# Strided sparse attention with a feed-forward layer: three normalizations on other engines, layer 1 begun with the strided pairs, transposes in two PSUM tiles

## The chip, the core and the metric

The kernel runs on one core of a Trainium2 chip. The core has five engines, each with its own queue, which it works through in order: TensorE (PE in the profile; PEld is its weight load), VectorE (DVE), ScalarE (ACT), GpSimd (POOL) and SyncE (SP). Sixteen DMA engines move data between HBM and the on-chip memory (SBUF); TensorE writes to PSUM, of which there are eight banks. [...] The metric is the device time of one execution in microseconds, median of several runs.

## The reference

```python
# q, k, v: 8 batches x 8 heads x 576 positions x 64; float32
scores = q @ k.T / sqrt(64)
rel = pos[:, None] - pos[None, :]
mask_local   = (rel >= 0) & (rel < 32)                                    # heads 0 to 3
mask_strided = (rel >= 0) & (pos[None, :] % 32 == pos[:, None] % 32)      # heads 4 to 7
attn = softmax(where(mask, scores, -1e9))
x = (attn @ v).transpose(0, 2, 1, 3).reshape(4608, 512)
h = x @ w_in                                      # 512 -> 2048
g = maximum(h, 0) + alpha * minimum(h, 0)         # alpha per column of h
out = g @ w_out                                   # 2048 -> 512
```

## The kernel before

**Attention.** Each batch has two units: the strided heads (4 to 7) and the local heads (0 to 3), two pairs of heads each. In the numbering of the code a batch's unit 0 is local (pairs `hp` 0 and 1) and its unit 1 is strided (pairs 2 and 3). Work is cut into pieces, and `pieces` (filled by `alone` and the loop at L559) is their order. A piece is one of:

- `T(u, "q")` or `T(u, "k")` (L234, `transpose_piece`): eight 128x128 transposes on TensorE, whose result is copied to `qT` or `kT`. For batches 0 and 1 ("early") the copy is done in two halves, one by VectorE and one by ScalarE. A k piece also has the last 64 positions (`tails`, L268), which it transposes first in the early batches.
- `Sc(g, i)` (L341) or `Sb(g)` (L290): half of the scores of pair g, or both halves. Scores go to PSUM, ScalarE takes the exponential into `et`. Every first half uses the double bank `sp`, of which there is one; every second half uses two of the banks that `hbank` deals out. In batch 0 the mask is added in PSUM by a matmul; in batch 1 VectorE multiplies by it (`run_masks`, L333), two pieces later or when the values of the pair want it.
- `Pv(g, a)` (L452): a group of the product with V, with one more column that holds the sum of the weights; then the normalization: on VectorE a reciprocal of the sums (L478) and a multiply (L480) into `x16`.
- `X(g)` (L485): transposes of `x16`, copied into `xT`, the input of layer 1. `xT[:, hp]` holds the 128 columns of pair `hp`, so the four k-slices (`kk`) of layer 1 are the four pairs.

**The feed-forward part** takes chunks of 512 tokens. `lin1_piece(n, m)` (L642) makes 128 of 2048 columns: four matmuls (`kk` 0 to 3) into a bank from `hbank`, a negative Relu on ScalarE (L662) and a combination on VectorE (L665), deferred by one step in `late`. There are three banks, `hb0` to `hb2`; the third joins the rotation (`turn`) when layer 1 begins. `lin2_piece(n, i)` (L671) is a quarter of a 128-token block: four matmuls; the fourth quarter ends with a copy `osb` on ScalarE (L684) and a store. From chunk 2 on layer 2 is done by `lin2_sums` (L738) with sums of quadrants in place of some products; the sums of weights are made once (`w_sums`, L699), the third of them at step 20 of chunk 2.

**Order.** Every instruction stays in the order of the program on its engine. The program begins with loads and with batch 0's pieces alone (loop at L890, 26 pieces); `warm` puts fillers between them, matmuls of zeros whose result nobody reads. Then come 16 pieces of layer 1 of chunk 0, then 16 parts of layer 2 of chunk 0 with batch 1's 22 pieces between them, as a list of numbers says (L930). From chunk 1 on the pieces of the next batch are spread over both layers.

**Buffers.** The pool `ps` has three PSUM banks for transposes, tails, values and outputs. A bank is given on when all its readers are done. `x16` has three buffers, `neg` (the negative Relu's output) three, `rc` (reciprocals) four.

**Queues for loads.** GpSimd issues most loads (L123 to L180, and the weights in `load_w`, L816) in the order of the program, between its own casts and copies: `cast_l` (float32 to float16 of the local q and k), `cast_v` (V of the strided heads), `over_v` (L202: an overlap of 32 positions between the blocks of local V).

The softmax here doesn't subtract the row's maximum and nothing guards it: scores larger than these inputs give would overflow.

## Time and profile before

| | |
|---|---|
| median of 7 runs | 305.46 us (305.21 to 306.19) |
| the profiled execution's own time | 305.46 us |
| its span | 303.6 us |
| TensorE busy | 295.1 us (97%) |
| VectorE, ScalarE, GpSimd busy | 221.9, 177.6, 170.4 us |
| granted TensorE clock | full in all of the 40 slices |
| layer 1 of chunk 0 | from 24.30 to 38.06 us |
| layer 2 of chunk 0, with batch 1's attention | from 38.06 to 61.15 us |

A row of the profile's groups reads: line, engine, operation, output and inputs, shape, count, busy time, mean of one, idle time before and what ended most of it. A line of the timeline has start, duration, engine, line, operation and the idle time of that engine before it with its releaser. The ends of matmuls are modelled; a run of them starts one about every 0.22 us (512 columns) though a single one is shown with 0.38.

### The profile page before, as it was taken

The numbers are of one execution on the slowest core, as the hardware profiler recorded it, in microseconds if no ns is written. First come the engines' busy times: TensorE is split into PE (matmuls) and PEld (weight loads), VectorE is DVE, ScalarE is ACT, GpSimd is POOL, SyncE is SP. The second block draws the span as 40 slices with busy tenths as digits, with TensorE's granted clock in tenths as the row PEclk, the third lists the DMA queues.
The fourth block names the chain that finished last, engine by engine and source line by source line (L and its number), as shares of the span: only waits on it lengthen the run. The fifth ranks groups of instructions, "written<-read, shape, count | busy, mean of one in ns | idle before, by whom it ended". The sixth has DMA issues, their size and how long they took to land.

```text
span 303.6 us, 7042 instructions
## 1 busy us (share of the span) xinstructions
PE 295.1 (97%) x2786; PEld 191.4 (63%) x2786; DVE 221.9 (73%) x417; ACT 177.6 (59%) x330; POOL 170.4 (56%) x176
## 2 busy tenths in 40 slices
PE   8799999999999999999999999999999999999995
PEld 3454455644555468746888887458845874684484
DVE  5686867758783889488848884888578958845872
ACT  3655764597547774677567765766477246516620
POOL 8872279847999874877397729771746003101300
PEclk9999999999999999999999999999999999999999
DMA  7999999999799982999399919961921080012004
GB/s 226 193 206 207 204 231 221 168 170 262 152 162 208 196 106 38 164 278 121 45 170 275 114 29 153 184 86 30 189 64 23 0 162 0 2 69 72 0 0 140
DMA packets 81201, 40.38 MB, mean 133 GB/s; under 512 B 58624, under 2 KB 76304, under 8 KB 81168
## 3 DMA queue, kind: packets, MB, share of 16 engines
q0 software_dynamic: 41728, 17.38, 48.6%
q1 hardware_dynamic: 39168, 22.03, 32.6%
q8 instruction: 22, 0.36, 0.6%
q10 hardware_dynamic: 272, 0.52, 0.5%
q14 instruction: 11, 0.09, 0.1%
HBM read 38.01 MB, written 9.44 MB: 156 GB/s over the span
## 4 chain that ended last, share of the span: by engine, by line
PE 87%; DVE 6%; DMA 2%; ACT 2%; issue 1%; SPq 0%; ACTq 0%
PE hb L652 41%; PE hb L771 25%; PE hb L679 8%; PE pv L469 4%; PE tp L250 2%; DMA kl<-in_k_dram 2%; PE sp L421 2%; PE opl L771 1%; DVE gsum L723 1%; DVE x L480 1%; PE xp L488 1%; DVE qT L190 1%; PE sph L421 1%; ACT kT L188 1%; PE hb L829 1%
## 5 line engine op out<-in xcount | busy, mean ns | idle before, releaser
L652 PE MATMUL hb<-xT,win 128*128 128x512 f16 (+1 forms) x640 | 132.0, 358 | 0.1
L665 DVE SCALAR_TENSOR_TENSOR gT<-neg,oma,hb 128x512 f16<-128x512 f32 x144 | 105.4, 744 | 36.2 <-ACT neg L662 28.3
L662 ACT ACTIVATE neg<-hb 128x512 f32<-128x512 f32 x144 | 86.0, 598 | 36.4 <-PE hb L652 35.8
L652 PEld LDWEIGHTS <-win 128*128 128x128 f16 x640 | 60.0, 98 | 54.6 <-issue 0.4
L436 POOL TENSOR_TENSOR et<-et,consts 128x576 f16<-128x576 f16 (+1 forms) x24 | 30.6, 1276 | 41.9 <-ACT et L434 41.8
L723 POOL TENSOR_TENSOR gsum<-gT 128x512 f16<-128x512 f16 x21 | 24.1, 1148 | 52.0 <-DVE gT L665 52.0
L771 PEld LDWEIGHTS <-gsum 128*128 128x128 f16 x448 | 41.6, 98 | 4.9 <-DVE gsum L723 0.2
L771 PEld LDWEIGHTS <-gT 128*128 128x128 f16 x336 | 31.5, 98 | 4.8
L480 DVE TENSOR_TENSOR x<-pv,rc 96x384 f16<-96x384 f32 (+2 forms) x62 | 33.0, 532 | 2.1
L443 POOL TENSOR_TENSOR et<-et,consts 128x576 f16<-128x576 f16 (+1 forms) x24 | 32.7, 1364 | 2.2 <-ACT et L440 2.2
L679 PE MATMUL hb<-wout,gT 128*128 128x512 f16 x128 | 32.3, 379 | 0.1
L469 PEld LDWEIGHTS <-et 72*128 72x128 f16 (+1 forms) x448 | 23.6, 98 | 10.9 <-issue 1.3
L783 ACT COPY o<-hb 128x512 f32<-128x512 f32 (+1 forms) x28 | 15.8, 565 | 24.1 <-PE hb L771 24.1
L771 PE MATMUL hb<-wout,gT 128*128 128x256 f16 x216 | 27.3, 273 | 0.0
L771 PE MATMUL hb<-wout,gsum 128*128 128x256 f16 x216 | 26.9, 273 | 0.0
L434 ACT ACTIVATE et<-sp 128x576 f16<-128x576 f32 (+1 forms) x24 | 15.5, 645 | 18.3 <-PE sp L421 18.3
L771 PE MATMUL hb<-wsum,gsum 128*128 128x256 f16 x216 | 26.0, 272 | 0.0
L786 DVE TENSOR_TENSOR o<-hb,o 128x512 f32<-128x512 f32 (+1 forms) x21 | 14.3, 679 | 14.7 <-PE hb L771 10.9
L478 DVE RECIPROCAL rc<-pv 72x6 f32<-72x6 f32 (+2 forms) x80 | 14.6, 182 | 10.0 <-PE pv L469 9.6
L440 ACT ACTIVATE et<-sph 128x288 f16<-128x288 f32 (+1 forms) x48 | 18.9, 409 | 0.0
L679 PEld LDWEIGHTS <-gT 128*128 128x128 f16 x128 | 10.7, 97 | 9.1
L469 PE MATMUL pv<-vs,et 72*128 72x65 f16 x256 | 15.5, 193 | 0.7 <-DVE vs L190 0.4
(103 smaller groups left out, 321.3 us busy)
## 6 DMA issues: line engine op xcount, KB each, us to landing
out_dram<-o SPq DMA_DIRECT2D x27, 256.0 KB, 3.8
kl<-in_k_dram SPq DMA_DIRECT2D x6, 512.0 KB, 8.4
ql<-in_q_dram SPq DMA_DIRECT2D x5, 512.0 KB, 8.2
stv<-in_v_dram POOLq DMA_DIRECT2D x8, 288.0 KB, 7.6
vl<-in_v_dram POOLq DMA_DIRECT2D x6, 384.0 KB, 10.0
win<-in_moe_w_in_dram POOLq DMA_DIRECT2D x4, 512.0 KB, 11.8
wout<-in_moe_w_out_dram POOLq DMA_DIRECT2D x4, 512.0 KB, 14.2
out_dram<-osb SPq DMA_DIRECT2D x8, 256.0 KB, 4.8
```

Of the source, the lines that this page charges most:

```text
L436: keep(nc.gpsimd.tensor_tensor(mv, mv, m, op=ALU.mult))
L440: keep(nc.scalar.activation(ev[:, n * y : n * y + n], sps[y][0:r, 0:n], AF.Exp, scale=SCALE))
L443: keep(nc.gpsimd.tensor_tensor(mv, mv, m, op=ALU.mult))
L469: keep(nc.tensor.matmul(pv[:, 65 * x : 65 * x + 65], et[0:r, c : c + 128], v16[0:r, 2 * P.pr + hh, t, :] if P.strided else v16[:, 6 * (2 * ...
L480: keep(nc.vector.tensor_tensor(P.x16[0:w, c0 : c0 + 64 * nb].rearrange("r (c e) -> r c e", e=64), pvv[:, :, 0:64], rc[0:w, 0:nb].unsqueeze ...
L652: keep(nc.tensor.matmul(hps[:, dst : dst + w], win16[:, kk, 128 * m : 128 * m + 128], xT[:, kk, src : src + w], start=(kk == 0 and x == 0) ...
L662: keep(nc.scalar.activation(neg, hps, AF.Relu, scale=-1.0))
L665: keep(nc.vector.scalar_tensor_tensor(gTs[n][:, m, :], neg, oma[:, m : m + 1], hps, op0=ALU.mult, op1=ALU.add))
L679: keep(nc.tensor.matmul(ops, gTs[n][:, kf, 128 * mt : 128 * mt + 128], wout16[:, kf, :], start=(kf == 0), stop=(kf == 15)))
L723: keep(eng.tensor_tensor(o[:, k0:k1], x[:, k0:k1], y[:, k0:k1], op=op))
L771: keep(nc.tensor.matmul(dst, lhs[:, kf, 128 * mt : 128 * mt + 128], rhs[:, kf, :], start=(first and own and kf == 0), stop=(kf == 7), skip ...
L783: keep(nc.scalar.copy(o, x))
```

## The change

1. *Transposes.* In batches 0 and 1 the eight transposes of a piece go into two PSUM tiles of four, and the copies are cut the same way: one engine copies the first four transposes for both pairs, the other the last four. Before, both engines read one tile, each for one pair.
2. *Normalizations.* In batch 0 the groups (pair 2, group 1), (pair 3, group 0) and (pair 0, group 0) are copied from PSUM to SBUF by ScalarE; the reciprocal stays on VectorE, the multiply is done by GpSimd. Both are put behind the next value piece's own normalization or ahead of the next output piece.
3. *Order of batch 0's pieces.* Local scores and values are interleaved differently, and the strided pairs' outputs come earlier.
4. *Layer 1.* In the last pieces of batch 0, layer 1's slices 2 and 3 (the strided pairs) of its first three column blocks are issued, then slice 0 of these; slice 1 follows in `lin1_piece`. The third bank joins before that. Four single fillers are left in the loop where there were fourteen.
5. *GpSimd's queue.* It casts both halves of batch 0's strided V, does `over_v` in two parts, and issues three of four output-weight loads and the loads of batch 1 behind the loop.
6. *Layer 2 of chunk 0.* The list of piece numbers is changed.
7. *Weight sum.* The third sum of weights is made in four quarters at steps 19, 21, 22 and 23.

```diff
@@ -199,10 +199,10 @@
                       "p (h t d) -> p h t d", h=2, t=8))
         cast16[(b, True, "v")] = v16
 
-    def over_v(b, eng):
+    def over_v(b, eng, lo=1, hi=24):
 
         v16 = vls[b % 2]
-        cast_copy(eng, v16[0:32, 1:24, :], v16[96:128, 0:23, :])
+        cast_copy(eng, v16[0:32, lo:hi, :], v16[96:128, lo - 1 : hi - 1, :])
 
 
     class Pair:
@@ -243,26 +243,26 @@
         dst = qTs[u % 2][:, :, 0:576] if nm == "q" else kTs[u % 2][:, :, 32:608]
         if early and nm == "k":
             tails(b, u, strided)
-        tp = pspool.tile([128, 8, 64, 2], F16, tag="ps", name="tp")
-        for j in range(8):
-            blk = (src[:, j % 2, 128 * (j // 2) : 128 * (j // 2) + 128] if strided
-                   else src[:, j].rearrange("p f d -> p (f d)"))
-            keep(nc.tensor.transpose(tp[:, j].rearrange("r p e -> r (p e)"), blk, ident))
-        if strided:
-            main = tp.rearrange("r j p e -> r e j p")
-            o = dst.rearrange("r e (j p) -> r e j p", j=8)[:, :, :, 0:64]
-        else:
-            main = tp.rearrange("r t p e -> r e p t")
-            o = dst[:, :, 0:512].rearrange("r e (p t) -> r e p t", t=8)
-        if early:
-            for e in range(2):
-                eng = "dve" if (nm == "q") == (e == 0) else "act"
-                if u == 0 and nm == "q":
-                    eng = "dve"
-                cast_copy(eng, o[:, e : e + 1], main[:, e : e + 1])
-            return
-        cast_copy("act", o, main)
-        if nm == "k":
+        halves = 2 if early else 1
+        nj = 8 // halves
+        for z in range(halves):
+            tp = pspool.tile([128, nj, 64, 2], F16, tag="ps", name="tp")
+            for x in range(nj):
+                j = nj * z + x
+                blk = (src[:, j % 2, 128 * (j // 2) : 128 * (j // 2) + 128] if strided
+                       else src[:, j].rearrange("p f d -> p (f d)"))
+                keep(nc.tensor.transpose(tp[:, x].rearrange("r p e -> r (p e)"), blk, ident))
+            if strided:
+                main = tp.rearrange("r j p e -> r e j p")
+                o = dst.rearrange("r e (j p) -> r e j p", j=8)[:, :, nj * z : nj * z + nj, 0:64]
+            else:
+                main = tp.rearrange("r t p e -> r e p t")
+                o = dst[:, :, 0:512].rearrange("r e (p t) -> r e p t", t=8)[:, :, :, nj * z : nj * z + nj]
+            eng = "act"
+            if early and (u == 0 and nm == "q" or (nm == "q") == (z == 0)):
+                eng = "dve"
+            cast_copy(eng, o, main)
+        if nm == "k" and not early:
             tails(b, u, strided)
 
     def tails(b, u, strided):
@@ -474,15 +474,33 @@
             late.pop(0)()
         w = P.w
         rc = rpool.tile([128, 8], F32, tag="rc", name="rc")
+        c0 = 128 * grp[0]
+        by_pool = P.b == 0 and (P.hp, a) in ((2, 1), (3, 0), (0, 0))
+        if by_pool:
+            st = npool.tile([128, 512], F32, tag="neg", name="pvs")
+            keep(nc.scalar.copy(st[0:w, 0 : 65 * nb], pv[0:w, 0 : 65 * nb]))
+            pv = st
         pvv = pv[0:w, 0 : 65 * nb].rearrange("r (c e) -> r c e", e=65)
-        keep(nc.vector.reciprocal(rc[0:w, 0:nb], pvv[:, :, 64]))
-        c0 = 128 * grp[0]
-        keep(nc.vector.tensor_tensor(
-            P.x16[0:w, c0 : c0 + 64 * nb].rearrange("r (c e) -> r c e", e=64),
-            pvv[:, :, 0:64],
-            rc[0:w, 0:nb].unsqueeze(2).to_broadcast([w, nb, 64]), op=ALU.mult))
+
+        def norm():
+            keep(nc.vector.reciprocal(rc[0:w, 0:nb], pvv[:, :, 64]))
+            keep((nc.gpsimd if by_pool else nc.vector).tensor_tensor(
+                P.x16[0:w, c0 : c0 + 64 * nb].rearrange("r (c e) -> r c e", e=64),
+                pvv[:, :, 0:64],
+                rc[0:w, 0:nb].unsqueeze(2).to_broadcast([w, nb, 64]), op=ALU.mult))
+
+        if not by_pool:
+            norm()
+        while later:
+            later.pop(0)()
+        if by_pool:
+            later.append(norm)
+
+    later = []
 
     def x_piece(P):
+        while later:
+            later.pop(0)()
         xp = pspool.tile([128, 1024], F16, tag="ps", name="xp")
         for t in range(P.n):
             keep(nc.tensor.transpose(
@@ -539,8 +557,12 @@
 
         if u0 == 1:
             fns = [T(u0, "q"), T(u0, "k"), Sc(A[0], 0), Sc(A[0], 1), T(u1, "q"), Sc(A[1], 0), T(u1, "k")]
-            fns += [Sc(A[1], 1), Sc(L[0], 0), Pv(A[0], 0), Sc(L[0], 1), Pv(A[0], 1), Pv(A[0], 2)]
-            fns += [Sc(L[1], 0), Pv(A[1], 0), Sc(L[1], 1), Pv(A[1], 1), Pv(A[1], 2)]
+            fns += [Sc(A[1], 1), Sc(L[0], 0), Pv(A[0], 0), Sc(L[0], 1), Pv(A[0], 1), Sc(L[1], 0)]
+            fns += [Pv(A[0], 2), Sc(L[1], 1), Pv(A[1], 0), Pv(A[1], 1), Pv(L[0], 0), Pv(A[1], 2)]
+            fns += [X(A[0]), Pv(L[0], 1), X(A[1]), Pv(L[1], 0), Pv(L[1], 1), X(L[0]), X(L[1])]
+            for fn in fns:
+                feed(fn, -1)
+            return
         else:
             fns = [T(u0, "q"), T(u0, "k"), Sb(A[0]), Sb(A[1])]
             fns += [Pv(A[0], 0), T(u1, "q"), Pv(A[0], 1), T(u1, "k"), Pv(A[0], 2), Sb(L[0])]
@@ -639,24 +661,35 @@
 
     gTs = {}
 
-    def lin1_piece(n, m):
-        if m == 0:
-            gTs[n] = gpool.tile([128, 16, 512], F16, tag="gT", name="gT")
+    hcur = {}
+
+    def lin1_mm(n, m, kks, first, last):
+        if first:
+            hcur[m] = hbank()
+        hps = hcur[m]
         c0 = (512 * n) % RING
         parts = [(c0, 0, min(512, RING - c0))]
         if c0 + 512 > RING:
             parts.append((0, RING - c0, 512 - (RING - c0)))
-        hps = hbank()
-        for kk in range(4):
+        for kk in kks:
             for x, (src, dst, w) in enumerate(parts):
                 keep(nc.tensor.matmul(
                     hps[:, dst : dst + w],
                     win16[:, kk, 128 * m : 128 * m + 128],
                     xT[:, kk, src : src + w],
-                    start=(kk == 0 and x == 0),
-                    stop=(kk == 3 and x == len(parts) - 1),
+                    start=(first and kk == kks[0] and x == 0),
+                    stop=(last and kk == kks[-1] and x == len(parts) - 1),
                     skip_group_check=True,
                 ))
+        return hps
+
+    def lin1_piece(n, m):
+        if m == 0:
+            gTs[n] = gpool.tile([128, 16, 512], F16, tag="gT", name="gT")
+        if n == 0 and m < 3:
+            hps = lin1_mm(n, m, (1,), False, True)
+        else:
+            hps = lin1_mm(n, m, (2, 3, 0, 1) if n == 0 else range(4), True, True)
 
         neg = npool.tile([128, 512], F32, tag="neg", name="neg")
         keep(nc.scalar.activation(neg, hps, AF.Relu, scale=-1.0))
@@ -696,7 +729,7 @@
 
         return wout16[:, 8 * i : 8 * i + 8, 256 * j : 256 * j + 256]
 
-    def w_sums(eng, which):
+    def w_sums(eng, which, k0=0, k1=8):
 
         w1, w2, w4 = wsum
         w3 = wq(0, 1)
@@ -708,7 +741,7 @@
         }
         for z in which:
             o, x, y, op = steps[z]
-            keep(eng.tensor_tensor(o, x, y, op=op))
+            keep(eng.tensor_tensor(o[:, k0:k1], x[:, k0:k1], y[:, k0:k1], op=op))
 
     def g_sum(eng, n, which, k0, k1):
 
@@ -873,12 +906,10 @@
     cast_l(0, "k")
     load_w(2, False)
     load_w(3, False)
+    cast_v(0, 0, "pool")
     cast_v(0, 1, "pool")
-    over_v(0, "pool")
-    for c in range(4):
-        load_w(c, True)
-    load_unit(1, True)
-    load_unit(1, False)
+    load_w(0, True)
+    over_v(0, "pool", 1, 12)
 
     warm(12)
     keep(nc.vector.tensor_copy(id16, ident[0:16, 0:16]))
@@ -892,13 +923,21 @@
             keep(nc.tensor.transpose(apt[:, 0:16], alpha_r, id16))
             keep(nc.vector.tensor_scalar(
                 oma, apt[:, 0:16], -1.0, 1.0, op0=ALU.mult, op1=ALU.add))
-        if i == 8:
-            cast_v(0, 0, "dve")
         attn_step(end0)
         if i < 2:
             warm(4 - i)
-        elif i > 8 and i not in (10, 13, 15):
+        elif i in (9, 11, 13, 16):
             warm(1)
+        if i == 13:
+            over_v(0, "pool", 12, 24)
+        if i == 21:
+            turn.append(2)
+        if i in (22, 23, 24):
+            lin1_mm(0, i - 22, (2, 3), True, False)
+    for c in range(1, 4):
+        load_w(c, True)
+    load_unit(1, True)
+    load_unit(1, False)
 
     def attn_n(n, end):
         for _ in range(n):
@@ -921,13 +960,14 @@
     cast_l(2, "k")
 
 
-    turn.append(2)
+    for m in range(3):
+        lin1_mm(0, m, (0,), False, False)
     for m in range(16):
         lin1_piece(0, m)
         attn_n(0, end1)
     for i in range(16):
         lin2_piece(0, i)
-        attn_n((0, 1, 1, 1, 1, 2, 1, 2, 1, 2, 1, 2, 2, 3, 2, 0)[i], end1)
+        attn_n((0, 0, 0, 1, 1, 2, 2, 2, 2, 2, 2, 2, 2, 2, 2, 0)[i], end1)
         if i > 13:
             attn_n(1, end1 + 2)
     assert pos["i"] == end1 + 2
@@ -954,8 +994,9 @@
                     w_sums(nc.vector, ({18: 1, 22: 2, 26: 4}[i],))
             else:
                 lin2_sums(n, i - 16)
-                if n == 2 and i == 20:
-                    w_sums(nc.vector, (3,))
+                if n == 2 and i in (19, 21, 22, 23):
+                    k0 = {19: 0, 21: 2, 22: 4, 23: 6}[i]
+                    w_sums(nc.vector, (3,), k0, k0 + 2)
             if n < B - 2 or i < 16 or i > 19:
                 acc += left / (22.5 if n == 1 else 16 if n == B - 2 else 20.5) * (0.5 if i < 16 else 1.0)
             cnt = int(acc)
```

## The prediction

> **What bounds the kernel now.** I read the page first.
>
> ```profile
> span 303.6 us, 7042 instructions
> ...
> PE 295.1 (97%) x2786; PEld 191.4 (63%) x2786; DVE 221.9 (73%) x417; ACT 177.6 (59%) x330; POOL 170.4 (56%) x176
> ```
>
> TensorE is the bound overall, but fillers count as busy there, so I cut the span at the stage borders with the table of stretches.
>
> ```profile
> 10.00:24.30 14.30, 12.81 (x190) 8.06 (x191) 10.48 (x28) 8.12 (x18) 10.10 (x14) 1.00 1.60 184
> 24.30:38.06 13.76, 13.76 (x64) 6.27 (x64) 10.66 (x15) 8.96 (x15) 3.79 (x6) 1.00 1.25 205
> 38.06:61.15 23.09, 22.18 (x262) 13.06 (x260) 15.96 (x38) 13.07 (x28) 19.52 (x22) 1.00 1.46 207
> 61.15:94.80 33.65, 33.65 (x297) 16.89 (x296) 23.59 (x43) 22.96 (x45) 26.28 (x24) 1.00 1.17 190
> ...
> 107.50:118.50 11.00, 10.69 (x115) 8.15 (x113) 10.10 (x18) 7.86 (x16) 5.26 (x6) 1.00 0.60 72
> ```
>
> The columns are stretch, sum, then PE, PEld, DVE, ACT, POOL. From 61.15 PE is full, but for 107.5 to 118.5. So the change can act in three places: the front (batch 0's attention, to 24.30), the shared stage (layer 2 of chunk 0 with batch 1's attention, 38.06 to 61.15), and near 118. What is gained or lost before 61.15 passes to the end undamped.
>
> In the front the timeline (start, duration, engine, line, what, idle before and its releaser) shows who is last:
>
> ```profile
> 15.78 0.19 DVE L478 RECIPROCAL rc<-pv 72x6 f32<-72x6 f32 x1 [0.43 <-PE pv L469]
> ...
> 23.79 0.46 DVE L190 COPY xT<-xp 128x576 f16<-128x576 f16 x1 [0.40 <-PE xp L488]
> ...
> 25.15 0.60 ACT L662 ACTIVATE neg<-hb 128x512 f32<-128x512 f32 x1 [1.44 <-PE hb L652]
> ...
> 25.78 2.48 DVE L665 SCALAR_TENSOR_TENSOR gT<-neg,oma,hb 128x512 f16<-128x512 f32 x3 [1.53 <-ACT neg L662]
> ```
>
> Between 15.78 and 23.41 VectorE runs ten normalizations almost without gap: 0.19 + 0.55 us for 384 elements, 0.17 + 0.42 for 256, so 8 x 0.73 + 2 x 0.59 = 7.0 of 7.6 us. It bounds the front. Layer 1 then takes 63 matmuls of 0.2184 from 24.30 to 38.06; the first piece's bank is free again at 25.78 + 0.74 (mean of the L665 row) = 26.5, just before the fourth piece's first matmul (24.30 + 11 x 0.2184 = 26.7).
>
> The timeline of the shared stage, and one line of the third place:
>
> ```profile
> 41.00 0.59 ACT L188 COPY qT<-tp 128x512 f16<-128x512 f16 x1 [2.30 <-DVE qT L190]
> ...
> 43.26 0.65 ACT L316 ACTIVATE et<-sp 72x576 f16<-72x576 f32 x1
> ...
> 43.80 0.70 ACT L320 ACTIVATE et<-hb 72x288 f16<-72x288 f32 x2
> ...
> 44.37 0.30 PE L308 MATMUL sp<-qT,kT 64*128 64x72 f16 x8
> ...
> 48.81 0.61 PE L250 MATMUL tp<-consts,kl 128*128 128x128 f16 x8 [0.35 <-ACT qT L188]
> ...
> 118.50 0.36 PE L469 MATMUL pv<-vs,et 72*128 72x65 f16 x6 [0.31 <-DVE x16s L480]
> ```
>
> The reader sees copies that wait for copies, exponentials that are 0.65 and 0.70 long, and TensorE idle behind ScalarE (0.35) and behind VectorE (0.31). The shared stage's PE work is 64 x 0.2165 (layer 2) + 4 x 0.45 and two tails of 0.17 (transposes) + two transposes of batch 2 (1.0) + 4 x 0.41 (scores) + 10 x 0.18 (values) + 4 x 0.26 (outputs) = 21.5; so 1.6 of 23.09 is stall. The two scores of a pair stand one layer-2 part apart (42.89, 44.37), and that part hides the exponentials.
>
> **What the Trainium skill says.** PSUM — Partial Sum Buffer, "PSUM bank collisions raise a hardware error": two engines must not touch one bank and quadrant at once, reads included. The trace agrees: ScalarE's half of a transpose's copy starts after VectorE's has ended (40.27 + 0.69, then 41.00); such waits sum to 5.6 and 4.2 us. GPSIMD Engine Reference, section 3, is used as a price below, with ScalarE: Activation LUTs, "What ACT_TABLE_LOAD costs": 186 ns + 0.833 per element; the trace's 512-element copy takes 0.59 where this gives 0.61.
>
> **The change, part by part.**
>
> *Transposes in two tiles.* The same matmuls and copies; the halves' copies no longer wait for each other (0.6 us each), but each half spans both heads of the pair, so scores now wait for both halves, where before the first pair waited for one. And a q and k transposition now takes five tiles (q, q, tail, k, k) of the three "ps" buffers instead of three. In the front, VectorE is held by ks and madd until 8.12 as before, its q half ends 8.80, tails 9.06; k's second half ends 10.02 against ScalarE's 10.15 before: first scores 10.05, gain 0.15. For the local unit: q halves from 11.7 (4 transposes are enough, before 12.09) to 12.95, k by 14.0, scores 14.03 against 14.34.
>
> *Cast of V to GpSimd.* 0.41 us off VectorE; on GpSimd 1.06 from 13.25 to 14.31, the other half to 15.37. First values at 14.6 instead of 15.40. Two split overlap copies (1.43 together) cost nothing: the first ends about 16.9, values of local pairs start at 18.4.
>
> *Three normalizations moved, new order.* Each takes 0.55 off VectorE and puts a copy on ScalarE (390 elements: 0.50, between the rows 0.59 for 512 and 0.41 for 288) and a multiply on GpSimd. The trace has no such multiply: masks of 576 take 1.28, sums of 512 1.15, so 2.0 ns per element and 0.12 fixed, 0.89 for 384; the GPSIMD page's 4497 ns for 2048 gives an estimate of 0.84. Range 0.8 to 1.3. Walking the queues from 14.6: scores of the second local pair end 17.67; its exponentials hold ScalarE to 18.45; only behind them comes the copy for the second moved one, 18.95; reciprocal behind VectorE's own work, 19.2; GpSimd has done the first multiply (17.7 to 18.6) and the second overlap copy (19.35), so this multiply is 19.35 to 20.25. That one is late next: pair 3's transposes 20.3 to 20.72, its copy to 21.4, the first new layer-1 group waits for that to 21.45, and the last pair's values, normalization (22.7), transposes (23.45) and copy (23.96) queue behind it. Without any such wait TensorE's own work from 14.2 on (4 fillers and six layer-1 matmuls, 10 x 0.217; 3 score halves x 0.58; ten values, 2.3 by the chain's 0.12 to 0.35; four outputs, 1.5: 7.7, where ten fillers fewer are minus 2.17 and the six plus 1.30) would end at 21.95. I take: nine layer-1 matmuls done and the last ones starting at 24.1, against 24.30.
>
> *Layer 1 with strided pairs first.* Saves no matmul, but 8 of the 63 behind 24.30, 1.75. That isn't all gained: three pieces finish within 0.65 and the fourth waits for the first's bank: 0.22 + 0.2 + 0.60 + 0.03 + 0.75 = 1.8 behind 24.1. Then 13 pieces x 0.866 = 11.25: end 37.2. Gain 38.06 - 37.2 = 0.9 (0.66 from the order, 0.2 from the start).
>
> *Loads behind the loop.* Three output-weight loads and ten of batch 1 (q, k, two tails and V of each unit) now issue behind GpSimd's last multiply (21.15) instead of from 18.3. The rows with "<-DMA win" and "<-DMA wout" (24.18, 26.71, 29.30, 31.83) show that the queue lands one weight load each 2.5 us in order, and the last weight load landed at 36.9. It is full until 29.30 with loads issued earlier, so the order and times of landing stay: nothing. Without that cover each us late would move batch 1's k (39.5).
>
> *Attention pieces in layer 2: (0,0,0,1,1,2,...).* Batch 1's start moves from part 1 to part 3: 37.2 + 4 x 0.87 = 40.7, against 39.63. Then both scores of a pair stand together: the second's first group needs the first exponential out of the double bank, 0.65 behind; its second needs the two banks, until 44.50 by the pattern 42.89/43.80/0.70. That is 1.0 us of stall which the part hid before. The next transposes come one part closer: k's first tile waits for q's VectorE half, behind masks and a normalization (0.75), its second for a normalization (0.5), against 0.35 and two short waits of 0.1 before: 0.7 more. The parallel copies and the missing wait for osb (43.41) give 0.2 back. Sum: +1.5 (0.5 to 2.0). With -0.9 that puts 61.15 at 61.8.
>
> *Weight sum in quarters.* Instead of one of 1.21 at 116.68, four of 0.43 (row of 512 elements). The idle 0.31 at 118.50 goes. But the last quarter stands behind the addition of its own part (119.83, 0.69), so ends about 120.6, while the group that reads it reaches the last two slices at 120.1: 0.5. Net +0.2 (-0.4 to +0.5).
>
> Sum: -0.9 + 1.5 + 0.2 = +0.8. The profiled execution took 305.46 (span 303.6 and 1.9 around), which is also the median. Forecast 306.3.
>
> **Rivals.** *The front is faster than my walk* (other side). If the moved copy and multiply aren't last, the last layer-1 matmuls can start as early as 22.6 (21.95 and three matmuls). Then layer 1 ends at 35.7, -2.4, and -2.4 + 1.5 + 0.2 = -0.7, 304.8. From a start before 23.3 on the change gains. For: in my walk GpSimd idles from 16.9 to 17.7, so it has room, and VectorE is no longer full. Against: ScalarE's queue of exponentials and copies.
> *The doubled pieces cost nothing.* If banks come free in another order than I take, +1.5 shrinks to 0.5: -0.9 + 0.5 + 0.2 = -0.2, 305.3, no change. Against: the exponentials' durations.
> *GpSimd becomes the bound.* At 1.3 per multiply, the second and third end 0.8 later; nothing hides it, as pair 3's transposes stand in front of all other TensorE work: +1.6, 307.1. For: VectorE masks took 2.02 a pair instead of 0.81 beside GpSimd casts. Against: the normalization's VectorE operand is in PSUM.
>
> **How the numbers follow.** About 0.2% (0.6 us) is what this kernel's measurement tells from no change. My forecast 0.45 (own range 305.7 to 307.0; a tenth of this lies within 0.2%), doubled pieces free 0.20, front faster 0.22 , GpSimd bound 0.13. Slower: 0.40 + 0.13 = 0.53; same 0.05 + 0.19 = 0.24; faster 0.22 + 0.01 = 0.23. Low end 304.3: the front case with the shared stage at +1.0. High end 307.4: GpSimd's case and a little of the unknown pattern of the copies.
>
> **What would show it.** The first layer-1 matmul that completes a piece at 24.1, an idle of about 1.2 before the fourth piece, layer 2 from 37.2; a wait of scores for ScalarE's exponentials of about 1 us near 45; transposes waiting for VectorE near 49; layer 1 of chunk 1 at 61.8; a wait on L711's successor near 120. I am wrong if the border at 61.15 moves forward, or if pair 3's transposes aren't kept by GpSimd.

## The result and the profile after

The changed kernel takes 306.96 us (median of 27 executions, 306.59 to 311.04) against 305.30 us before (median of 64). The ratio is 1.0082 with a 95% interval of 1.0065 to 1.0099. It lies above that of the medians (1.0054) because it follows the means, 308.05 against 305.55 us (the latter without two slow executions of 310.09 and 314.86). The executions of the changed kernel fall into groups that differ in the TensorE clock they were granted over the span.

| mean granted clock | executions | time |
|---|---|---|
| 0.998 and more | 15 | 306.59 to 307.11, median 306.82 |
| 0.992 to 0.994 | 8 | 308.31 to 309.77, mean 308.9 |
| 0.988 to 0.989 | 4 | 310.79 to 311.04 |

Below, an execution is at full clock when this mean is 0.998 or more. The kernel before is at full clock in all but one of the 84 executions that were measured beside the experiments. So two things are to be explained: 1.5 us at full clock (306.82 - 305.30), and some 2.1 us more for each step down in clock.

The profiled execution is one of the group with the lowest clock (311.04 us). The head of the page, TensorE's row and the granted clock:

```profile
span 309.3 us, 7033 instructions
...
PE 296.3 (96%) x2776; PEld 192.7 (62%) x2776; DVE 219.9 (71%) x416; ACT 178.5 (58%) x333; POOL 173.2 (56%) x181
...
PEclk9998999899999999999999999999999999999999
```

TensorE is busy 1.2 us longer than before though it runs ten instructions fewer, and two of the 40 slices, the fourth (23 to 31 us) and the eighth (54 to 62 us), are below full clock. The table of stretches finds where (columns: stretch, sum, PE, PEld, DVE, ACT, POOL with counts, granted clock, DMA share, GB/s):

```profile
10.00:24.30 14.30, 12.29 (x180) 8.18 (x180) 7.68 (x23) 8.85 (x20) 12.72 (x17) 0.92 1.54 182
24.30:38.06 13.76, 12.66 (x62) 5.85 (x61) 10.00 (x14) 8.45 (x15) 4.86 (x9) 0.96 1.25 205
38.06:61.15 23.09, 20.16 (x209) 11.15 (x207) 14.20 (x32) 10.95 (x26) 17.94 (x21) 0.93 1.52 193
...
18.55:21.98 3.43, 1.92 (x40) 1.36 (x37) 2.65 (x10) 2.12 (x5) 3.29 (x5) 1.00 1.24 205
21.98:25.40 3.42, 3.42 (x24) 2.04 (x23) 1.00 (x4) 0.64 (x1) 3.42 (x6) 0.50 1.25 209
...
50.00:52.00 2.00, 0.20 (x5) 0.08 (x2) 2.00 (x3) 0.53 (x1) 2.00 (x2) 1.00 1.27 342
52.00:54.00 2.00, 1.59 (x10) 0.92 (x10) 1.39 (x5) 0.75 (x2) 2.00 (x4) 0.67 0.87 148
54.00:56.00 2.00, 2.00 (x20) 1.15 (x19) 0.73 (x3) 0.28 (x1) 1.96 (x4) 0.50 2.10 134
```

From 21.98 to 25.40 TensorE has half its clock, right behind 3.43 us in which it was busy for only 1.92. The same follows the stretch from 50 to 52, in which it was busy for 0.20 of 2.00.

The timeline of the front (start, duration, engine, line, operation, idle before it and its releaser):

```profile
20.66 0.43 PE L506 MATMUL xp<-consts,x 72*128 72x72 f16 x8 [0.85 <-POOL x L487]
...
21.82 0.48 PE L676 MATMUL hb<-xT,win 128*128 128x512 f16 x1 [0.33 <-ACT xT L510]
...
27.79 11.38 PE L676 MATMUL hb<-xT,win 128*128 128x512 f16 x52 [1.10 <-DVE gT L698]
```

Pair 3's transposes wait for GpSimd's multiply, and the fourth piece of layer 1 waits 1.10 us for VectorE to empty the first piece's bank. The timeline of the shared stage:

```profile
46.56 0.31 PE L308 MATMUL sp<-qT,kT 64*128 64x72 f16 x8 [0.61 <-ACT et L316]
...
49.40 2.04 DVE L329 TENSOR_TENSOR et<-et,consts 72x576 f16<-72x576 f16 x2
49.52 1.61 POOL L192 COPY vl<-vl 32x1495 f16<-32x1495 f16 x1
...
52.10 0.38 PE L254 MATMUL tp<-consts,kl 128*128 128x128 f16 x4 [1.90 <-DVE qT L190]
...
52.79 0.61 PE L254 MATMUL tp<-consts,kl 128*128 128x128 f16 x4 [0.31 <-DVE x L487]
```

The scores wait for the exponentials, and the k transposes wait 1.90 and 0.31 us for VectorE. VectorE is late because two masks take 2.04 us while GpSimd copies `vl`. In the kernel before, the same pair of masks took 0.81:

```profile
46.73 0.81 DVE L329 TENSOR_TENSOR et<-et,consts 72x576 f16<-72x576 f16 x2
```

The third place, in the changed kernel:

```profile
124.42 0.69 DVE L819 TENSOR_TENSOR o<-hb,o 128x512 f32<-128x512 f32 x1 [0.16 <-PE hb L804]
...
125.03 1.00 DVE L744 TENSOR_TENSOR wout<-wout 128x512 f16<-128x512 f16 x1
...
126.08 0.38 PE L804 MATMUL hb<-wout,gsum 128*128 128x256 f16 x2 [0.92 <-DVE wout L744]
```

TensorE waits 0.92 us for the last quarter of the weight sum, which takes 1.00 us, where the other three take 0.41 and 0.75 for two.

### The profile page after: what moved, and what is told of

Read it like the earlier page. It is cut to its first block, busy times and chain, and to the rows that moved or that the text cites. A ratio compares the mean times of both kernels' runs of the same rounds, so it can differ in the third digit from the quotient of the medians.

```text
span 309.3 us, 7033 instructions
## 1 busy us (share of the span) xinstructions
PE 296.3 (96%) x2776; PEld 192.7 (62%) x2776; DVE 219.9 (71%) x416; ACT 178.5 (58%) x333; POOL 173.2 (56%) x181
## 4 chain that ended last, share of the span: by engine, by line
PE 91%; DVE 4%; DMA 2%; ACT 1%; POOL 1%; issue 0%; SPq 0%; DVEq 0%; ACTq 0%
PE hb L676 41%; PE hb L804 27%; PE hb L712 9%; PE pv L469 4%; PE tp L254 3%; DMA kl<-in_k_dram 2%; PE sp L421 2%; PE xp L506 1%; PE opl L804 1%; PE sph L421 1%; DVE x L487 1%; DVE qT L190 1%; DVE et L329 1%; POOL x L487 1%; PE hb L862 0%
## 5 line engine op out<-in xcount | busy, mean ns | idle before, releaser
L676 PE MATMUL hb<-xT,win 128*128 128x512 f16 (+1 forms) x640 | 133.8, 360 | 1.4 <-DVE gT L698 1.1
L436 POOL TENSOR_TENSOR et<-et,consts 128x576 f16<-128x576 f16 (+1 forms) x24 | 30.9, 1286 | 46.6 <-ACT et L434 46.5
L756 POOL TENSOR_TENSOR gsum<-gT 128x512 f16<-128x512 f16 x21 | 24.1, 1148 | 52.0 <-DVE gT L698 52.0
L712 PE MATMUL hb<-wout,gT 128*128 128x512 f16 x128 | 33.0, 388 | 0.0
L487 DVE TENSOR_TENSOR x<-pv,rc 96x384 f16<-96x384 f32 (+2 forms) x59 | 31.3, 530 | 2.0
L443 POOL TENSOR_TENSOR et<-et,consts 128x576 f16<-128x576 f16 (+1 forms) x24 | 31.4, 1310 | 2.2 <-ACT et L440 2.2
L469 PEld LDWEIGHTS <-et 72*128 72x128 f16 (+1 forms) x448 | 24.1, 99 | 10.7 <-issue 1.2
L816 ACT COPY o<-hb 128x512 f32<-128x512 f32 (+1 forms) x28 | 15.8, 565 | 24.1 <-PE hb L804 24.1
L192 POOL COPY vs<-stv 72x1024 f16<-72x1024 f16 x16 | 16.4, 1050 | 1.1 <-DMA stv<-in_v_dram 1.1
```

What stands on the lines that cost most here:

```text
L192: keep(nc.gpsimd.tensor_copy(o, i))
L436: keep(nc.gpsimd.tensor_tensor(mv, mv, m, op=ALU.mult))
L443: keep(nc.gpsimd.tensor_tensor(mv, mv, m, op=ALU.mult))
L469: keep(nc.tensor.matmul(pv[:, 65 * x : 65 * x + 65], et[0:r, c : c + 128], v16[0:r, 2 * P.pr + hh, t, :] if P.strided else v16[:, 6 * (2 * ...
L487: keep((nc.gpsimd if by_pool else nc.vector).tensor_tensor(P.x16[0:w, c0 : c0 + 64 * nb].rearrange("r (c e) -> r c e", e=64), pvv[:, :, 0:64],
L676: keep(nc.tensor.matmul(hps[:, dst : dst + w], win16[:, kk, 128 * m : 128 * m + 128], xT[:, kk, src : src + w], start=(first and kk == kks ...
```

## Experiments

Each kernel is one edit, or a few, of the kernel before or of the changed kernel, and each computes the whole result (fillers are no part of it). Ratios are against the kernel before, measured beside it. "The border" is the time at which layer 1 of chunk 1 begins (61.15 us before), and "a fall" is a stretch in which TensorE gets half its clock. The theory: at full clock the loss is the list of pieces in layer 2 and the weight sum, and the rest is the clock, which falls where TensorE is left idle. Rivals: the transposes' five tiles, the moved normalizations, or a chip that merely differs.

### The changed kernel once more

No edit.

> The changed kernel as it is, to have an execution of it beside the others. Theory C (clock): its executions fall into groups by the granted TensorE clock, about 306.8 us at a clock of 1.00, and 2 and 4 us more where TensorE ran 3 to 4 us at half clock, once (0.994) or twice (0.988). Rival D (loads or waits make the longer ones, the clock only follows): longer executions also at a clock of 1.00.

Measured: 308.11 us (306.93 to 309.1, 6 executions), ratio 1.0086 (1.0069 to 1.0103). One execution has clock 0.994; the five at full clock spread from 306.93 to 309.1, much wider than the 306.59 to 307.11 of the first measurement. Three of these five take 308.1 and more, which theory C doesn't allow and the rival does. So the clock isn't the only thing that varies between executions.

### Fillers put back

```diff
         elif i in (9, 11, 13, 16):
             warm(1)
+        elif 17 <= i < 24:
+            warm(2 if i < 20 else 1)
```

> The changed kernel with ten fillers put back behind pieces 17 to 23 (two behind 17, 18, 19, one behind the others), so 14 again. Theory C: TensorE's idle time between 18 and 22 us is what lets the clock fall there, so the half clock at 22 to 25 goes; the shortest executions stay at 306.8 (306.6 to 307.2, as the fillers lie in waits), and none has two falls (no 311). Rival D: the spread stays as in the changed kernel, and all are 0.5 to 2.2 longer by the fillers.

Measured: 308.28 us (307.12 to 309.74, 6), ratio 1.0096 (1.0071 to 1.0121). The time doesn't improve, and the fall of the profiled execution lies elsewhere. First the changed kernel's table of stretches, then this one's:

```profile
17.40:20.80 3.40, 2.22 (x49) 1.75 (x48) 2.70 (x10) 2.48 (x6) 2.66 (x4) 1.00 1.25 208
```

```profile
17.40:20.80 3.40, 3.40 (x58) 2.30 (x53) 2.17 (x9) 2.38 (x6) 2.74 (x4) 1.00 1.24 207
49.80:53.20 3.40, 2.23 (x24) 1.38 (x25) 2.45 (x7) 0.75 (x2) 3.35 (x5) 0.87 1.46 161
```

With the fillers TensorE is busy throughout 17.4 to 20.8 and the front of this profile keeps full clock. Its fall (clock 0.994) begins within 49.8 to 53.2, in the shared stage. No execution of the six shows two falls (none below 0.993), but two show one, against one of the six without the added fillers; so that fillers prevent falls isn't shown in this kernel. They also cost the front 0.2 us: from its first values piece to layer 2 go 23.08 us (14.81 to 37.89), against 22.84 (14.85 to 37.69) and 22.85 (14.61 to 37.46) in the profiles of the next two experiments, which have the same front without them at full clock.

### The old list of pieces

```diff
-        attn_n((0, 0, 0, 1, 1, 2, 2, 2, 2, 2, 2, 2, 2, 2, 2, 0)[i], end1)
+        attn_n((0, 1, 1, 1, 1, 2, 1, 2, 1, 2, 1, 2, 2, 3, 2, 0)[i], end1)
```

> The changed kernel with the old list of pieces in layer 2 of chunk 0. Theory L (the list costs: two scores of a pair side by side, and the second transposes one part closer): the shortest executions fall by 1.0 to 2.0, to 304.8 to 305.8, and the half clock near 53 us goes, so none has two falls. Rival T (the five tiles in three buffers cost, whatever the list): at most 0.4 less, 306.4, and TensorE still waits over 1 us for VectorE ahead of the k transposes.

Measured: 306.02 us (305.41 to 306.88, 12), ratio 1.0013 (1.0002 to 1.0025); eleven of the twelve are at full clock. This is the largest recovery by a single edit: 2.1 us in the median against the changed kernel measured beside it. Its chain (start, duration, engine, tile, line) and a stretch of its front:

```profile
37.69 1.73 PE hb L712 x8
...
61.18 2.60 PE hb L676 x12
```

```profile
18.50:21.90 3.40, 1.88 (x40) 1.37 (x37) 2.62 (x10) 2.12 (x5) 3.26 (x5) 1.00 1.24 204
```

Layer 2 begins at 37.69 and the border lies at 61.18. TensorE is as idle in the front as in the changed kernel's profile (busy for 1.88 of 3.40 us, against 1.92 of 3.43), but here the clock didn't fall.

### The weight sum in one piece

```diff
-                if n == 2 and i in (19, 21, 22, 23):
-                    k0 = {19: 0, 21: 2, 22: 4, 23: 6}[i]
-                    w_sums(nc.vector, (3,), k0, k0 + 2)
+                if n == 2 and i == 20:
+                    w_sums(nc.vector, (3,))
```

> The changed kernel with the third sum of weights in one piece at step 20, as before. Theory W: the last quarter, behind an addition, held TensorE 0.92 us near 126, and the one piece costs 0.31; so 0.6 less than the changed kernel at the same clock, 306.2. Rival: the wait only moves to the next bank, 0.0 to 0.2 less.

Measured: 307.38 us (306.03 to 308.54, 8), ratio 1.0058 (1.0039 to 1.0077). Three executions at 0.992 to 0.994 take 307.78 to 308.54; the five at full clock take 306.03 to 307.54. The fastest is 0.56 below the fastest of the changed kernel's first measurement, and 0.90 below the fastest of the one beside it, so 0.6 fits but isn't pinned down here.

Up to the weight sum this is the changed kernel, and its profile is at clock 0.999, so it serves as the changed kernel's front and shared stage at full clock. Its timeline:

```profile
23.52 1.45 PE L676 MATMUL hb<-xT,win 128*128 128x512 f16 x6
...
26.07 2.10 PE L676 MATMUL hb<-xT,win 128*128 128x512 f16 x9 [1.10 <-DVE gT L698]
...
44.84 0.31 PE L308 MATMUL sp<-qT,kT 64*128 64x72 f16 x8 [0.61 <-ACT et L316]
...
49.15 0.38 PE L254 MATMUL tp<-consts,kl 128*128 128x128 f16 x4 [0.66 <-DVE qT L190]
```

and two lines of its chain:

```profile
37.46 3.45 PE hb L712 x16
...
61.78 2.59 PE hb L676 x12
```

Layer 2 begins at 37.46, 0.60 earlier than before, and the stage behind it takes 61.78 - 37.46 = 24.32 instead of 23.09. The border comes 0.63 later. This profile is an early one: its first values piece starts at 14.61, where the other profiles of this front with two tiles have it at 14.79 to 14.92, so 0.60 is the upper end of what the front gains (0.37 in the profile with the old list).

### The new list alone

The kernel before with the list of the change.

```diff
-        attn_n((0, 1, 1, 1, 1, 2, 1, 2, 1, 2, 1, 2, 2, 3, 2, 0)[i], end1)
+        attn_n((0, 0, 0, 1, 1, 2, 2, 2, 2, 2, 2, 2, 2, 2, 2, 0)[i], end1)
```

> The kernel before with the new list of pieces alone. Theory L (the list costs by its doubled pieces): 1.0 to 1.5 more than before at full clock, 306.3 to 306.8, layer 1 of chunk 1 at 62.2 to 62.7 us, and TensorE waits about 0.6 us for the first exponential of pair 6; in a share of the executions the clock falls near 50 us. Rival T (five tiles in three buffers): the list alone costs at most 0.4.

Measured: 308.37 us (307.19 to 309.72, 6), ratio 1.0093 (1.0067 to 1.0119). The list alone costs as much as the whole change, and more than the 1.0 to 1.5 expected: 1.9 to 3.2 us in the three executions at full clock, 2.9 to 4.4 in the three at 0.994. Its chain:

```profile
38.06 3.45 PE hb L679 x16
...
48.60 1.76 DVE et L329 x2
...
65.32 2.59 PE hb L652 x12
```

The front is untouched (38.06 as before), but the border moves from 61.15 to 65.32, with slow masks on the chain at 48.60 and half clock behind them. So the list alone can make the clock fall, with all fillers in place.

### Fewer fillers alone

The kernel before with four fillers in the loop instead of fourteen.

```diff
-        elif i > 8 and i not in (10, 13, 15):
+        elif i in (9, 11, 14, 16):
             warm(1)
```

> The kernel before with 4 of its 14 single fillers between batch 0's pieces. Theory C (TensorE's idle time lets the clock fall): VectorE bounds this stretch, so at full clock nothing changes (305.3), but in a share of the executions TensorE runs at half clock for 3 to 4 us behind 20 us, and these are 1.5 to 2.5 longer. Rival D (the clock doesn't follow from fillers): all within 0.5 of before.

Measured: 307.44 us (306.32 to 308.52, 7), ratio 1.0059 (1.0038 to 1.008). All seven executions are at 0.989 to 0.994; of the 36 of the kernel before beside them, none is below 0.998. Stretches of this kernel, then of the kernel before:

```profile
18.50:21.90 3.40, 2.15 (x46) 1.59 (x44) 3.15 (x11) 1.99 (x4) 3.40 (x6) 1.00 1.24 206
21.90:28.70 6.80, 6.59 (x30) 2.96 (x30) 2.88 (x6) 1.83 (x3) 1.53 (x4) 0.50 1.24 206
```

```profile
18.50:21.90 3.40, 3.36 (x55) 2.17 (x54) 2.94 (x9) 1.84 (x5) 2.90 (x5) 1.00 1.25 207
```

Taking out matmuls that nobody reads leaves TensorE busy for 2.15 of 3.40 us, and its clock is half for the next 6.8 us. In the chain, 63 matmuls of layer 1 follow:

```profile
24.23 15.97 PE hb L652 x63
```

They take 15.97 instead of 13.76 us. The 2.2 us are what half clock takes away there: half of the 4.47 us from 24.23 to 28.70. So in this profile the ten fillers taken out gained 0.07 us (the chain enters layer 1 at 24.23 instead of 24.30) and cost 2.2 us of clock. The busy time that the profile shows can't be all that decides: of the two windows of 3.40 us at half clock, the second follows one (21.90 to 25.30) in which TensorE shows as busy for 3.19. The border lies at 64.28, 1.0 later still, under the old list: the second masks, late now at 48.87, meet GpSimd's copy and take 1.99.

### The weight sum in quarters alone

```diff
-    def w_sums(eng, which):
+    def w_sums(eng, which, k0=0, k1=8):
...
-                if n == 2 and i == 20:
-                    w_sums(nc.vector, (3,))
+                if n == 2 and i in (19, 21, 22, 23):
+                    k0 = {19: 0, 21: 2, 22: 4, 23: 6}[i]
+                    w_sums(nc.vector, (3,), k0, k0 + 2)
```

> The kernel before with the third sum of weights in four quarters alone. Theory W: 0.4 to 0.8 more, as the last quarter waits behind the addition of its part and TensorE for it (idle 0.9 on L711's release, in place of 0.31). Rival: within 0.2 of before.

Measured: 305.90 us (305.73 to 307.34, 22), ratio 1.002 (1.0012 to 1.0028): +0.59. Its timeline:

```profile
119.32 1.26 POOL L443 TENSOR_TENSOR et<-et,consts 128x576 f16<-128x576 f16 x1
...
119.87 1.00 DVE L711 TENSOR_TENSOR wout<-wout 128x512 f16<-128x512 f16 x1
...
120.92 0.38 PE L771 MATMUL hb<-wout,gsum 128*128 128x256 f16 x2 [0.92 <-DVE wout L711]
```

The last quarter runs beside a mask multiply on GpSimd, takes 1.00 us and holds TensorE for 0.92, where before the idle was 0.31: +0.61, the measured cost.

### What is left of the change

The changed kernel with the old list, the sum in one piece and the ten fillers (edits as shown above), and with one tile for batch 1's transposes.

```diff
-        halves = 2 if early else 1
+        halves = 2 if early and b == 0 else 1
...
-        attn_n((0, 0, 0, 1, 1, 2, 2, 2, 2, 2, 2, 2, 2, 2, 2, 0)[i], end1)
+        attn_n((0, 1, 1, 1, 1, 2, 1, 2, 1, 2, 1, 2, 2, 3, 2, 0)[i], end1)
```

> The changed kernel with the old list, the sum in one piece, ten fillers back, and two tiles in batch 0 alone (batch 1 has one tile and the old halves). If list, sum, tiles of batch 1 and clock are what costs, and the front gains 0.5 to 0.9: layer 2 of chunk 0 at 37.2 to 37.6, layer 1 of chunk 1 at 60.3 to 60.7, 304.4 to 304.9, and no half clock. If batch 1's loads or VectorE set the border at 61.15 instead: 305.2 to 305.5, no gain left.

Measured: 305.57 us (305.18 to 306.6, 14), ratio 1.0008 (0.9997 to 1.0019), all at full clock. Its chain:

```profile
26.54 11.38 PE hb L681 x52
37.92 1.73 PE hb L717 x8
...
61.13 2.59 PE hb L681 x12
```

Layer 2 begins 0.14 earlier than before and the border is where it was. The old list with the faster front (layer 2 at 37.69) gave 61.18. So under the old list what the front gains is lost again in the shared stage.

### One tile for the transposes

The changed kernel with the transposes and copies of the kernel before.

```diff
-        halves = 2 if early else 1
+        halves = 2 if early and False else 1
...
+            if early and halves == 1:
+                for e in range(2):
+                    eng = "dve" if (nm == "q") == (e == 0) or u == 0 and nm == "q" else "act"
+                    cast_copy(eng, o[:, e : e + 1], main[:, e : e + 1])
+                continue
```

> The changed kernel with one PSUM tile for a transposition and the old halves of the copy. From the old tiles under the new list (the border at 63 us or later) against the new tiles under it (61.8): two tiles help by 0.3 to 0.8, so this one takes 307.1 to 307.7 at full clock. Rival T (five tiles in three buffers cost): 0.3 to 0.8 less than the changed kernel, 306.0 to 306.5.

Measured: 307.65 us (306.88 to 309.72, 6), ratio 1.0085 (1.0054 to 1.0116). In its chain layer 2 begins at 37.82 and layer 1 of chunk 1 at 62.28, a stage of 24.46 against 24.32 with two tiles. The tiles aren't the cause; a difference under 0.4 us couldn't be told from one profile.

### No moved normalizations

```diff
-        by_pool = P.b == 0 and (P.hp, a) in ((2, 1), (3, 0), (0, 0))
+        by_pool = False
```

> The changed kernel with all ten normalizations of batch 0 on VectorE. If VectorE bounds the front without the move: the matmul group that completes layer 1's first pieces starts 0.4 to 1.2 later than 23.5, and 307.2 to 308.0 at full clock. Rival (GpSimd's and ScalarE's leg is as long as what it takes off): within 0.3 of the changed kernel, 306.5 to 307.1, and less idle TensorE near 20 us.

Measured: 308.53 us (307.98 to 310.14, 6), ratio 1.0114 (1.009 to 1.0139). A line of its chain, and one of its timeline:

```profile
23.98 1.04 PE hb L676 x4
```

```profile
48.32 1.54 DVE L329 TENSOR_TENSOR et<-et,consts 72x576 f16<-72x576 f16 x2
```

The group that completes layer 1's first pieces starts at 23.98, against 23.52 with the sum in one piece and 23.76 with the old list. Part of this is a later start: counted from the first values piece (14.88, 14.61 and 14.85), it comes after 9.10, 8.91 and 8.91 us. So the moved normalizations gain 0.2 us, less than the 0.4 to 1.2 expected. Layer 2 begins at 37.85 and the border is at 63.14: the stage takes 25.29 at full clock, 0.97 more than 24.32, with masks of 1.54 us where GpSimd copies. In its profile it is this, more than the normalizations themselves, that makes this kernel slower than the changed one.

### A list in between

The same reduced version with nine fillers in all and batch 1 begun one part later than before.

```diff
-        elif i in (9, 11, 13, 16):
+        elif i in (9, 11, 13, 16) or 17 <= i < 22:
...
-        attn_n((0, 0, 0, 1, 1, 2, 2, 2, 2, 2, 2, 2, 2, 2, 2, 0)[i], end1)
+        attn_n((0, 0, 1, 1, 1, 2, 1, 2, 1, 2, 2, 2, 2, 3, 2, 0)[i], end1)
```

> The changed kernel with the sum in one piece, one tile in batch 1, nine fillers (five put back), and a list that starts one part later than the old one, with no pair of scores side by side: (0,0,1,1,1,2,1,2,1,2,2,2,2,3,2,0). If batch 1's loads and casts set its pace, a later start loses nothing and the front's gain stays: layer 1 of chunk 1 at 60.6 to 61.0, 304.7 to 305.1. If the pieces behind it are too close: 305.3 to 306.0.

Measured: 305.48 us (305.12 to 306.79, 14), ratio 1.0001 (0.9988 to 1.0014). Layer 2 begins at 37.64 and the border lies at 60.89, 0.26 earlier than before, and the span of this profile is 303.3 instead of 303.6; but the median is that of the kernel before (305.42 beside it). So a later start without two scores side by side costs nothing, and no version measured has a lower median than the kernel before.

### The copy of V's overlap out of the masks' way

The changed kernel with one GpSimd copy behind the loads that followed it.

```diff
-    over_v(1, "pool")
     load_v(2, False)
     load_d(2)
     load_v(2, True)
+    over_v(1, "pool")
```

> The changed kernel with one GpSimd copy moved: the overlap copy of batch 1's local V is issued behind the five loads that stood after it, so that it starts near 52.5 instead of 49 to 49.5. Theory (masks slide into that copy): under the new list the masks of batch 1's second strided pair start at 48 to 49.4 and take 1.5 to 2.0 us when they meet the copy and 0.81 when they don't; this makes the executions at full clock scatter up to 2 us and leaves TensorE idle long enough for a fall of its clock at 52 to 56. Then here these masks take 0.81 to 1.0, the first wait of the k transposes for VectorE is 0.7 or less instead of 1.90, no half clock shows between 50 and 57, and executions at full clock lie at 306.8 or below with little scatter, median 306.5 to 307.0 (half clock near 22 to 25 stays, at 308 to 309). Rival (loads and casts of batch 1 set the pace, the masks only follow): full-clock executions still scatter from 306.8 to 308.5 and falls at 52 to 56 stay, median 307 to 308.5. Against both: the copy now delays the casts of batch 2's local q and k by nothing, or the local values of batch 1 wait for it near 55; then a wait for GpSimd shows there, up to 1 us slower.

Measured: 308.06 us (307.65 to 308.46, 5), ratio 1.0084 (1.0071 to 1.0098). Timeline, chain and stretch:

```profile
49.43 0.81 DVE L329 TENSOR_TENSOR et<-et,consts 72x576 f16<-72x576 f16 x2
...
50.90 0.38 PE L254 MATMUL tp<-consts,kl 128*128 128x128 f16 x4 [0.67 <-DVE qT L190]
```

```profile
39.21 3.45 PE hb L712 x16
...
63.53 2.59 PE hb L676 x12
```

```profile
49.80:53.20 3.40, 2.42 (x37) 1.59 (x35) 2.70 (x8) 1.34 (x3) 3.29 (x5) 1.00 2.00 151
```

In the trace the theory holds: with the copy away the masks start at the same time (49.43) but take 0.81 instead of 2.04, the wait falls from 1.90 to 0.67, the stage is 24.32, as in the undisturbed profile, and its clock stays full (the fall of this profile is in the front). In the times it fails: the two executions at full clock take 307.65 and 307.84, not 306.8 or less. So the copy is what makes the masks slow. That the collision leads to the second fall fits (none of the five has two), but five executions don't show it, and it isn't all of the spread at full clock.

## Why the prediction was right and wrong

It was right in direction and wrong in size: +0.8 was forecast, the ratio of 1.0082 is +2.5.

**Front, -0.9: right in mechanism, -0.4 to -0.6 in size.** The fourth piece idled 1.10 (1.2 forecast), and the multiply took 0.82 (0.89 forecast from the trace, and 0.84 estimated from the GPSIMD page). Pair 3's transposes did wait for GpSimd. The group of six at 23.52 is slice 0 of three pieces and then the last slices, which so begin at 23.52 + 3 x 0.217 = 24.17, as forecast (24.1). From there to the fourth piece went 1.90 instead of 1.8, and the 52 matmuls behind took 11.38 instead of 11.25, so layer 2 began at 37.46, not 37.2, in the early profile, and at 37.69 in another. The rival in which the front is 2.4 faster is excluded, and the one in which GpSimd takes 1.3 a multiply as well. The loads moved behind the loop cost nothing that shows: GpSimd's cast of batch 1's local k starts at 45.03 under the new list at full clock, against 44.57 before, but at 44.44 in the reduced version, which moves them too.

**Shared stage, +1.5: right in mechanism, +1.23 at full clock with undisturbed masks.** 61.8 was forecast for the border and 61.78 measured, but that close a hit is luck: the front gained 0.3 less than forecast and the stage cost 0.3 less, and the profile is an early one. The stall of the scores behind ScalarE shows as 0.61 (1.0 forecast), the k transposes' waits as 0.66 and 0.31 (0.75 and 0.5). What the forecast didn't see is that the new list brings the second pair of masks to where GpSimd copies `vl`: 1.54 to 2.04 us in the four profiles under the new list that start them at 48.1 to 49.4, 1.00 in one at 49.28, 0.81 in the two that had begun them by 48.04, and 0.81 again at 49.43 once the copy was moved. It is the time that decides and not the list itself: with fewer fillers alone, they start at 48.87 under the old list and take 1.99. The rival that the doubled pieces cost nothing falls with the old list, which alone gives back 2.1 us, and with the list in between, which starts later than the old one but keeps the scores apart and costs nothing. The prediction used the slow masks (2.02 beside casts) as evidence about GpSimd's own multiply, and not as the price of a mask that is moved.

**Weight sum, +0.2 (-0.4 to +0.5): too small, +0.6.** The term that failed is the last quarter's 0.43: it took 1.00 beside a GpSimd multiply. The wait for it was 0.92, not 0.5. The Trainium skill, SBUF — State Buffer, "Who interferes with whom", says that a VectorE instruction with two SBUF inputs contends with a GpSimd instruction that reads SBUF; both of these slow VectorE operations are of that kind and both traces agree (0.41 to 1.00, 0.81 to 2.04). That the multiply is the cause rests on this for the quarter: no run moved it, but the three quarters that take 0.41 and 0.75 for two begin while GpSimd is idle. The collision could be read from the profile before: GpSimd multiplies there from 118.10 and from 119.34, 1.27 us each, and the forecast put the end of the quarter at 120.6.

**The step that failed most: the clock, put at nothing.** In "ten fillers fewer are minus 2.17" the fillers were counted as TensorE work that disappears, and the shared stage's longer waits only as waits. Both make the clock fall: without the ten fillers alone it fell in seven executions of seven, and with the new list alone, all fillers in place, in three of six. The Trainium skill, TensorE: Matmul & The Clock Gate, Part 1, says that the clock falls to half after an idle window of about 3.4 us, and that the windows run free of the kernel. The falls here are that long (3.42 us, and 6.8 us for two), and free windows would explain why a kernel with unchanged order falls in 12 executions of 27; no run shows it. But TensorE wasn't idle for such a time ahead of them: it was busy for 1.92 of 3.43 us, and 2.15 of 3.40 with fewer fillers alone. Here the measurement decides: a window that is idle in part can be enough.

The 15 executions at full clock average 306.82 and all 27 average 308.05, so executions with a fall are worth 1.2 of the 2.5 us between the means. Not all of that is clock: half clock for 3.42 us takes away 1.71 us at most, and a step was 2.1. A fall in the front costs 1.44: from the first values piece to layer 2 go 24.27 to 24.29 us in the three profiles of this front that have one, and 22.84 and 22.85 in the two that don't. The shared stage of the profiled execution takes 27.04 instead of 24.32, and 1.24 of these 2.72 us is the longer wait behind the slow masks (1.90 against 0.66).

**The sum.** At full clock: border +0.63 and weight sum +0.61 make 1.24 of the 1.5 measured, where +0.8 was forecast. A front that starts 0.2 to 0.3 later than in the early profile, as in the others, would give the rest. Executions with falls add 1.2 to the mean. The border of the profiled execution is 4.44 later than at full clock (66.22 against 61.78), and its span 4.2 to 4.3 longer than the 305.0 to 305.1 of full clock.

**What stays open.** Why some executions at full clock take 308 and more (the changed kernel once more, the new list alone, the moved copy) isn't known. Slow masks alone can do it in part: without the moved normalizations they cost 0.97 at a clock of 1.0. But with the copy moved, and the masks fast in its profile, the executions at full clock still took 307.65 and 307.84, and no profile fell on one of the longest. Why the clock falls in one execution and not in another with the same idle time isn't known either. What paces the shared stage, so that a front up to 0.4 earlier isn't seen at its end under the old list, was not tried; batch 1's loads and casts on GpSimd are a guess. For it speaks that the cast of its local q begins at 42.42 before and in the reduced version, and at 41.83 in the list in between, whose border is earlier.

## What to carry to other kernels

Before taking out work that only keeps TensorE busy, count TensorE's busy share in each stretch of some 3.4 us without it: a stretch at 56 to 63% was followed by half clock here in part or all of the executions. Look at the waits that a change adds in the same way. When an instruction is moved, look at what the other engines do at its new time: a VectorE operation with two inputs from SBUF took up to two and a half times as long beside GpSimd here. And an earlier start is worth only what the stage behind can take, so follow it to the next border before counting it.

## What the runs showed of the hardware

- Half clock came behind windows in which TensorE was busy for 56 and 63% of the time. No single gap in them is longer than 0.85 us. In the kernel before, busy for 3.36 of 3.40 us, it didn't come. A fall of 3.42 us at the start of layer 1 cost 1.44 us, and one of 6.8 us, of which 4.47 lay in layer 1, 2.2.
- A fall isn't certain: fewer fillers alone fell in seven executions of seven, the changed kernel in 12 of 27 and again in one of six, and with the old list, though TensorE is as idle in the front (1.88 of 3.40 us busy, 18.5 to 21.9), in one of 12.
- Two masks of 72x576 take 0.81 us alone and up to 2.04 beside a GpSimd copy, which took 1.61 itself in that run and 1.42 in the others, whether it met masks or not; and a sum of 512 f16 columns 0.41 alone and 1.00 beside a GpSimd multiply.
- GpSimd multiplies 72x384 f32 in 0.82 us, and ScalarE copies 72x390 in 0.48.
